# A wait of its own where a matmul pair swaps PSUM banks, a score round moved under it, and row maxima turned by two 64-row transpositions

## The chip, the cores and the metric

The kernel runs on one core of one Trainium2 chip. The metric is the time of one execution in microseconds of the device. The kernel before took 2326.66 us (median of three runs, 2324.75 to 2327.2). Its profiled execution took 2327.55 us.

## The reference

Two blocks work on 2048 tokens of width 576 in float32, and a gate per token mixes them:

```
x = A_x;  g = sigmoid((x * gate_w).sum(-1))
qkv = x @ wqkv                  # 32 heads of width 18
p   = softmax(q k^T * 18**-0.5);   a = (p v) @ wo
y   = layernorm(B_x);  h = gelu(y @ w1 + b1);   b = h @ w2 + b2   # 576 -> 4608 -> 576
out = g * a + (1 - g) * b
```

The attention's input A_x and the perceptron's input B_x are different arrays.

## The kernel before

**Precision and array shapes.** Products are made from float32 parts split in two (`hh` and `hl`, high and low), so that most products take three matmuls. Three shapes of the TensorE array occur in the main loop. Scores and both perceptron products use 64 rows by 128 columns: two matmuls, one on the upper and one on the lower 64 rows, run side by side and write different PSUM banks. The product of probabilities and values (PV, line 268) uses 128 rows by 32 columns. The transposition of line 219 has 128 rows by 32 columns as well.

**The main loop.** There are 32 units (a pair of heads, half of the queries). A unit has 16 steps (`kc`), one for each 128 keys, which makes 512 steps. The maximum of each row of scores must be known before its exponentials, so scores are made twice:

- A *round* (`s1_round`, matmuls on line 202) makes 128x512 scores for two heads, in two banks of the pool `ps_s1`. That pool has three banks, taken in turn. VectorE (DVE) takes each bank's maxima (line 204). A unit has 32 rounds; they run `LEAD` = 4 rounds and a whole unit ahead of the loop.
- When a unit's 32 rounds are done, `s1_finish` (lines 212 to 215) joins the maxima on DVE. `rows` transposes them (line 219), ScalarE (ACT) copies them out of PSUM (line 221), and four DMAs put them as extra rows beside the queries, so that later scores come out with the maximum subtracted.
- `s2` (line 251) makes the scores of one step for one of two blocks of queries, in the one pair of banks of `ps_s2`. ACT takes the exponential (line 253). The next `s2` must wait for that, since there is no second pair of banks.
- `pv` (line 268) multiplies two steps' probabilities with the values, every second step.

**The perceptron as filling.** Between these, `fill` takes pieces from a generator `mlp`: three pieces in two steps, numbered 0 (even step), 1 and 2 (odd step). A generator of `h_pair` makes two chunks of the hidden layer (27 pairs of matmuls on line 489, then DVE line 511 and ACT line 512 read the two banks out and GpSimd and ACT make the GELU). One of `out_pair` makes the second product for 128 tokens (24 pairs on line 614). In `out_pair` the upper 64 rows write bank 0 and the lower 64 rows write bank 1 for 12 pairs (`turn` 0); then they swap (`turn` 1). At that point the kernel calls `nc.tensor.drain()` (line 603), so that no row group writes into a bank that the other is still writing. While rounds last, one `out_pair` is spread over the three pieces as 7, 8 and 9 pairs, so the swap lies inside piece 1, five pairs in. After the last pair, DVE adds the banks to the sum (line 593).

**Order.** The order of instructions on each engine is the order in which the Python code issues them; the pools only add waits. `next_round` issues one round. In an odd step a round stands at the start and one after piece 1; in an even step one stands at the start and one after the second `s2`. Four further rounds stand in steps 2, 4, 6 and 8. Before the loop, `between(n)` issues n stretches of the perceptron, and rounds stand between them.

In what follows R is a round, S an `s2`, V a `pv`, T the transposition, O pairs on line 614, H pairs on line 489.

Of the kernel before, what the change touches and what calls it, by code (L numbers as in the profile page):

```python
# [16 lines left out]
P = 128  # L17
# [11 lines left out]
G = 4  # L29
NFC = F // P  # L30
NG = NFC // G
ND = 288
# [7 lines left out]
LEAD = 4  # L40
# [18 lines left out]
def gated_mix_kernel(ctx: ExitStack, tc: tile.TileContext, x, wqkv, wo, w1, b1, w2, b2, gate_w, out):  # L59
    nc = tc.nc  # L60
# [18 lines left out]
    ident = const.tile([P, P], F32, name="ident")  # L79
# [12 lines left out]
    asm = ctx.enter_context(tc.tile_pool(name="asm", bufs=2))  # L92
    ps_s1 = ctx.enter_context(tc.tile_pool(name="ps_s1", bufs=NS1, space=PSUM))
# [5 lines left out]
    def psum(pool):  # L99
        return pool.tile([P, TB], F32, name="ps")  # L100
# [88 lines left out]

    M4 = {}  # L190

    def s1_round(u, r):


        t, kb = (r % 8, r // 8) if u == 0 else divmod(r, 4)
        if r == 0:
            M4[u] = asm.tile([P, 2, 8, 4], F32, name="m4")
        qa, ka = QA[u % 3], KA[UNITS[u][0] % 3]
        for h in range(2):
            r0 = 64 * h  # L200
            ps = psum(ps_s1)
            nc.tensor.matmul(ps, qa[r0:r0 + 54, t * P:(t + 1) * P], ka[r0:r0 + 54, kb * TB:(kb + 1) * TB],  # L202
                             start=True, stop=True)
            nc.vector.tensor_reduce(M4[u][:, h, t, kb:kb + 1], ps, axis=AX.X, op=ALU.max)  # L204

    def s1_finish(u):

        m4 = M4.pop(u)
        nm = asm.tile([P, 2, 8], F32, name="nm")
        nm2 = asm.tile([P, 2, 2, 8], F32, name="nm2")  # L210
        nmh = asm.tile([P, 2, 8], F32R, name="nmh")
        nc.vector.tensor_reduce(nm, m4, axis=AX.X, op=ALU.max, negate=True)
        nc.vector.tensor_copy(nmh, nm)
        nc.vector.tensor_copy(nm2[:, :, 0, :], nmh.bitcast(F32))
        nc.vector.tensor_tensor(nm2[:, :, 1, :], nm, nmh.bitcast(F32), op=ALU.subtract)

        def rows():
            ps = psum(ps_s1)
            nc.tensor.transpose(ps[:32, :P], nm2.rearrange("p a b c -> p (a b c)"), ident)
            mr = asm.tile([32, P], F32R, name="mr", bufs=1)  # L220
            nc.scalar.activation(mr, ps[:32, :P], AF.Copy)
# [21 lines left out]
    def s2(u, kc, qb):  # L243
        qa, ka = QA[u % 3], KA[UNITS[u][0] % 3]
        n = u * NT + kc
        if n < 2 and qb == 0:
            RING.insert(n, pp.tile([P, 2, 2, TB], F32, name="p"))
        ps = ps_s2.tile([P, 2, TB], F32, name="pss")
        for h in range(2):
            r0 = 64 * h  # L250
            nc.tensor.matmul(ps[:, h, :], ka[r0:r0 + 56, kc * P:(kc + 1) * P], qa[r0:r0 + 56, qb * TB:(qb + 1) * TB],  # L251
                             start=True, stop=True)
        nc.scalar.activation(RING[n % 3][:, qb], ps, AF.Exp, scale=SCALE)  # L253
# [47 lines left out]
    rounds = [(u, r) for u in range(NU) for r in range(NR)]  # L301
    rounds.reverse()

    ROWS = []
    looped = [False]

    def next_round():
        if rounds:
            u, r = rounds.pop()
            s1_round(u, r)  # L310
            if r == NR - 1:
                defer(1, lambda: s1_finish(u))


    def mlp():
        W1, W2, HT = {}, {}, {}
# [148 lines left out]
        def h_pair(q, last, inner=False):  # L465
# [46 lines left out]
            nc.scalar.activation(zs[0], ps[0], AF.Identity, bias=b[0])  # L512
# [70 lines left out]
        def out_pair(i, t, acc):  # L583

            tb, g = seq[i]
            tok = slice(t * P, (t + 1) * P)
            cs = [slice(nn * ND, (nn + 1) * ND) for nn in range(2)]
            bare = not rounds

            def add(ps, base):  # L590
                for nn in range(2):
                    dst = acc[:, t, cs[nn]]
                    nc.vector.scalar_tensor_tensor(dst, ps[nn][:, :ND], 0.5, b2b[:, cs[nn]] if base else dst,  # L593
                                                   op0=ALU.mult, op1=ALU.add)
            ps = [psum(free_pool()) for _ in range(2)]
            ends = {7, 15} if piece[0] == 0 else cuts(24, (3, 2, 1)[piece[0]])
            k = 0
            for turn in range(2):
                if turn == 1 and bare:
                    add(ps, g == 0)  # L600
                    ps = [psum(free_pool()) for _ in range(2)]
                elif turn == 1:
                    nc.tensor.drain()
                for j in ORDER:
                    while (i, j) not in HT:
                        cut[0] = 3
                        yield 0
                    hh, hl = HT[i, j]
                    w_ = ready(W2, (i * (G // 2) + j // 2, j % 2))
                    for h_, p_ in ((hh, 0), (hh, 1), (hl, 0)):  # L610
                        for h in (0, 1) if turn == 0 else (1, 0):
                            r = slice(64 * h, 64 * h + 64)
                            nn = h ^ turn
                            nc.tensor.matmul(ps[nn][:, :ND], h_[r, tok], w_[p_][r, cs[nn]],  # L614
                                             start=(k == 0 or bare and k == 3 * G), stop=(k == 6 * G - 1 or bare and k == 3 * G - 1))
# [419 lines left out]
    RING.append(ring2)  # L1035


    def out_proj():

        OT, BT, done, tmp = {}, {}, {}, {}  # L1040
# [174 lines left out]
    proj = out_proj()  # L1215
    over = [None]
# [29 lines left out]
    for u in range(NU):  # L1246
        for kc in range(NT):
            step = u * NT + kc
            if kc == 1:
                if u + 2 < NU:  # L1250
                    load_q(u + 2)
                if u % 2 == 0 and u // 2 + 1 < NPAIR - 1:
                    load_k(u // 2 + 1)
                    load_v(u // 2 + 1)
                elif u == NU - 5:
                    load_k(NPAIR - 1)
                elif u == NU - 4:
                    load_v(NPAIR - 1)
            at[0] = step

            next_round()
            s2(u, kc, 0)
            run_due(462.0)
            if kc % 2:
                fill(step, 1)
            elif step > 0:
                pv(step - 2)
                while ROWS:
                    ROWS.pop(0)()
                run_due(2080.0)  # L1270
                if step <= 2 * LEAD:
                    next_round()
            else:
                fill(step, 2)
            if kc % 2:
                next_round()
            s2(u, kc, 1)
            if kc % 2 == 0:

                next_round()  # L1280
            run_due(462.0)
            fill(step, 2 if kc % 2 else 0)
    pv(NSTEP - 2)
# [28 lines left out]
```

## Time and profile before

| | |
|---|---|
| time, median of three runs | 2326.66 us (2324.75 to 2327.2) |
| time of the profiled execution | 2327.55 us |
| its span, first to last instruction | 2325.8 us |
| TensorE matmuls | 2295.2 us busy, 99% |
| weight loads | 1615.4 us, 69% |
| DVE | 1663.7 us, 72% |
| ACT | 1379.9 us, 59% |
| GpSimd (POOL) | 947.8 us, 41% |
| matmuls of line 614 | 6912 |
| granted TensorE clock, mean | 0.997 |

PE stands for TensorE's matmuls, PEld for its weight loads. A matmul counts as busy from its start to its modelled end, and several overlap, so 99% does not say that TensorE is at its peak. What counts is how far apart the starts of matmuls lie. In a timeline the columns are start, duration of the merged row, engine, line, operation, output and inputs, form, and the number of instructions; in brackets, the idle time before and what ended it.

### The profile page before, as it was taken

To read this page: it belongs to the slowest core of one execution; us is meant where nothing else is said; L and a number is where in the kernel's file an instruction comes from. 1 tells how busy PE (TensorE), PEld (TensorE's weight loads), DVE (VectorE), ACT (ScalarE), POOL (GpSimd) and SP (SyncE) were. 2 spreads that over 40 slices of the span, in tenths; PEclk is the share of its full clock that TensorE was granted. 3 is DMA by queue.
4 is the path that set the end of the run, shared out by engine and by line. 5 is a ranking of instruction groups with operands and counts; after the bars stand their busy time and mean duration, and the time that the engine had idled before them with its cause. 6 is when DMAs were issued, how large, how long until landed. Compare 5 with 4: busy or idle time off the path is not lost.

```text
span 2325.8 us, 50689 instructions
## 1 busy us (share of the span) xinstructions
PE 2295.2 (99%) x20601; PEld 1615.4 (69%) x20601; DVE 1663.7 (72%) x2921; ACT 1379.9 (59%) x1631; POOL 947.8 (41%) x936
## 2 busy tenths in 40 slices
PE   8999999999999999999999999999999999999999
PEld 7878666666666666666666666666666666666669
DVE  5675777777777777777777777777777777777545
ACT  4223666666666666666666666666666666666662
POOL 4002466566553434443444344434434443333320
PEclk9999899999999999999999999999999999999999
DMA  7756545445473524232263324233364233322346
GB/s 242 247 190 197 175 144 170 157 136 169 139 187 131 164 86 127 96 118 96 90 174 144 114 94 134 81 118 116 118 162 153 94 118 107 106 97 101 113 139 223
DMA packets 160654, 323.58 MB, mean 139 GB/s; under 512 B 56062, under 2 KB 83618, under 8 KB 149586
## 3 DMA queue, kind: packets, MB, share of 16 engines
q1 hardware_dynamic: 156582, 313.57, 43.1%
q10 hardware_dynamic: 3840, 6.78, 0.8%
q8 instruction: 162, 2.65, 0.5%
q14 instruction: 70, 0.57, 0.1%
HBM read 229.07 MB, written 95.16 MB: 139 GB/s over the span
## 4 chain that ended last, share of the span: by engine, by line
PE 90%; POOL 3%; DVE 2%; issue 2%; DMA 1%; ACT 1%; SPq 0%; ACTq 0%; POOLq 0%; DVEq 0%
PE ps L614 20%; PE ps L268 19%; PE ps L489 17%; PE pss L251 12%; PE ps L202 11%; PE ps L880 4%; PE ps L1184 3%; PE ps L898 2%; POOL zz L159 1%; POOL w L159 1%; POOL hl L159 1%; DVE m L204 1%; DMA wraw<-in_B_w_dram 1%; PE ps L795 0%; DMA p<-in_A_wqkv_dram 0%
## 5 line engine op out<-in xcount | busy, mean ns | idle before, releaser
L204 DVE TENSOR_REDUCE m<-ps 128x1 f32<-128x512 f32 x2048 | 1297.3, 684 | 431.2 <-PE ps L202 429.7
L253 ACT ACTIVATE p<-pss 128x1024 f32<-128x1024 f32 x684 | 701.7, 1026 | 456.9 <-PE pss L251 445.3
L489 PE MATMUL ps<-big,w 64*128 64x512 f32 x3834 | 514.8, 392 | 0.1
L614 PE MATMUL ps<-w,hh 64*128 64x288 f32 x4352 | 501.2, 300 | 13.8 <-ACT z L512 2.1
L159 POOL TENSOR_SCALAR zz<-zz 128x512 f32<-128x512 f32 x272 | 169.3, 622 | 827.4 <-ACT zz L575 761.8
L251 PE MATMUL pss<-qa,ka 56*128 56x512 f32 x2048 | 484.1, 437 | 3.8 <-ACT p L253 1.1
L253 ACT ACTIVATE ring<-pss 128x1024 f32<-128x1024 f32 x340 | 348.9, 1026 | 231.4 <-PE pss L251 225.6
L202 PE MATMUL ps<-ka,qa 54*128 54x512 f32 x2048 | 460.8, 410 | 2.8 <-DVE m L204 1.2
L614 PEld LDWEIGHTS ps<-w,hh 64*128 64x128 f32 x4352 | 402.4, 186 | 68.9 <-issue 42.4
L489 PEld LDWEIGHTS ps<-big,w 64*128 64x128 f32 x3834 | 390.1, 185 | 59.6 <-ACT vt L909 0.3
L159 POOL TENSOR_TENSOR zz<-zz,z 128x512 f32<-128x512 f32 x280 | 361.4, 1291 | 35.6 <-ACT zz L577 10.5
L251 PEld LDWEIGHTS pss<-qa,ka 56*128 56x128 f32 x2048 | 198.0, 185 | 254.6 <-ACT p L253 121.4
L614 PE MATMUL ps<-w,hl 64*128 64x288 f32 x2176 | 351.7, 293 | 0.0
L268 PE MATMUL ps<-p,vt 128*32 128x512 f32 x2736 | 344.5, 598 | 0.0
L202 PEld LDWEIGHTS ps<-ka,qa 54*128 54x128 f32 x2048 | 244.5, 185 | 34.0 <-DVE m L204 12.1
L614 PEld LDWEIGHTS ps<-w,hl 64*128 64x128 f32 x2176 | 236.2, 186 | 0.5
L159 POOL TENSOR_TENSOR w<-x,w 128x576 fp32r<-128x576 f32 (+1 forms) x34 | 68.3, 2012 | 308.8 <-ACT w L385 304.6
L159 POOL TENSOR_TENSOR hl<-zz,hh 128x512 fp32r<-128x512 f32 x134 | 174.1, 1300 | 19.0 <-ACT hh L538 8.1
L268 PE MATMUL ps<-ring,vt 128*32 128x512 f32 x1360 | 179.1, 598 | 0.0
L268 PEld LDWEIGHTS ps<-p,vt 128*32 128x32 f32 x2736 | 71.4, 109 | 147.3 <-issue 147.3
L593 DVE SCALAR_TENSOR_TENSOR x<-ps,x 128x288 f32<-128x288 f32 x270 | 110.8, 452 | 29.8 <-PE ps L614 16.4
L880 PE MATMUL ps<-big,wqk 128*128 128x512 f32 x504 | 123.4, 399 | 0.1
(122 smaller groups left out, 1403.3 us busy)
## 6 DMA issues: line engine op xcount, KB each, us to landing
w<-w_scr SPq DMA_DIRECT2D x54, 1152.0 KB
w<-w_scr SPq DMA_DIRECT2D x108, 576.0 KB
w_scr<-w SPq DMA_DIRECT2D x18, 1152.0 KB
w_scr<-w SPq DMA_DIRECT2D x36, 576.0 KB
qa<-qk_scr SPq DMA_DIRECT2D x192, 72.0 KB
ka<-qk_scr SPq DMA_DIRECT2D x90, 144.0 KB
x<-in_B_w_dram SPq DMA_DIRECT2D x34, 288.0 KB
qk_scr<-hh SPq DMA_DIRECT2D x36, 256.0 KB
```

What stands on the lines that cost most here:

```text
L159: fn(*args, **kw)
L202: nc.tensor.matmul(ps, qa[r0:r0 + 54, t * P:(t + 1) * P], ka[r0:r0 + 54, kb * TB:(kb + 1) * TB], start=True, stop=True)
L204: nc.vector.tensor_reduce(M4[u][:, h, t, kb:kb + 1], ps, axis=AX.X, op=ALU.max)
L251: nc.tensor.matmul(ps[:, h, :], ka[r0:r0 + 56, kc * P:(kc + 1) * P], qa[r0:r0 + 56, qb * TB:(qb + 1) * TB], start=True, stop=True)
L253: nc.scalar.activation(RING[n % 3][:, qb], ps, AF.Exp, scale=SCALE)
L268: nc.tensor.matmul(OB[u][r:r + 32, :], v[:, k, 19 * h:19 * h + 32], RING[c % 3][:, qb, h, :], start=(k == 0), stop=(k == NT - 1))
L489: nc.tensor.matmul(ps[h], wt[w_][r, c, :], Y[s_][r, c, :], start=(k == 0), stop=(k == 26))
L593: nc.vector.scalar_tensor_tensor(dst, ps[nn][:, :ND], 0.5, b2b[:, cs[nn]] if base else dst, op0=ALU.mult, op1=ALU.add)
L614: nc.tensor.matmul(ps[nn][:, :ND], h_[r, tok], w_[p_][r, cs[nn]], start=(k == 0 or bare and k == 3 * G), stop=(k == 6 * G - 1 or bare and ...
L880: nc.tensor.matmul(ps, w_[:, c, ms], big[:, s_, :], start=(k == 0), stop=(k == len(prods) - 1))
L898: nc.tensor.matmul(ps[:, :ND], big[:, s_, tok], w_[:, c, cs], start=(k == 0), stop=False)
L1184: nc.tensor.matmul(ps[t, n][:, :ND], OT[b][3][:, s_, tok], w_part(w_, c)[:, cs], start=(c == 0 and k == 0), stop=(c == 4 and k == 1))
```

## The change

1. In `out_pair` the drain at the swap goes. The two last matmuls of turn 0 each add one to a semaphore `turn_sem`, and the first matmul of turn 1 waits for both. Just before that wait a round is issued (`lend_round`), if the swap isn't the end of a piece; the next round that the loop would issue is then left out (`loop_round`). This happens at all 137 swaps.
2. The maxima of a unit lie in one 128x128 tile with the values that `s1_finish` makes. Inside the loop, `rows` makes two transpositions, one for each 64 partitions, in the shape of the scores (64 rows by 128 columns), into two banks of `ps_s1`. DVE copies the 32 rows that matter out of each (line 224 of the kernel after). It is issued after the second `s2` of the even step, no longer after `pv`. One unit of 32, the one before the loop, is done as before.
3. One stretch of the perceptron fewer stands in the first `between`, and two rounds stand in place of the last `between(1)`. Of the four further rounds in steps 2 to 8, those in steps 6 and 8 go. Of the chunk pair number 2, DVE takes both read-outs (before, ACT took one).

```diff
     def rows():
-        ps = psum(ps_s1)
-        nc.tensor.transpose(ps[:32, :P], nm2.rearrange("p a b c -> p (a b c)"), ident)
         mr = asm.tile([32, P], F32R, name="mr", bufs=1)
-        nc.scalar.activation(mr, ps[:32, :P], AF.Copy)
+        if looped[0]:
+            for h in range(2):
+                half(mr, h)
+            store_rows(mr)
...
+    def half(mr, h):
+        r = slice(64 * h, 64 * h + 64)
+        ps = psum(ps_s1)
+        nc.tensor.transpose(ps[:, :64], nm2[r, :], ident[r, r])
+        nc.vector.tensor_copy(mr[:, r], ps[:32, :64])
...
+    def lend_round():
+        if rounds and not lent[0]:
+            next_round()
+            lent[0] = 1
+
+    def loop_round():
+        if lent[0]:
+            lent[0] = 0
+        else:
+            next_round()
...
-            nc.scalar.activation(zs[0], ps[0], AF.Identity, bias=b[0])
+            if q == 2:
+                nc.vector.tensor_scalar(zs[0], ps[0], b[0], None, op0=ALU.add)
+            else:
+                nc.scalar.activation(zs[0], ps[0], AF.Identity, bias=b[0])
...
                 elif turn == 1:
-                    nc.tensor.drain()
+                    if 3 * G not in ends:
+                        lend_round()
+                    turned[0] += 2
+                    nc.tensor.wait_ge(turn_sem, turned[0])
...
+                            if k == 3 * G - 1:
+                                mm.then_inc(turn_sem, 1)
...
-        between(6 if len(rounds) == NU * NR - NR else 2)
+        between(5 if len(rounds) == NU * NR - NR else 2)
         next_round()
         run_due(233.0)
-    between(1)
+    for part in range(2):
+        next_round()
+        run_due(500.0)
...
                 pv(step - 2)
-                while ROWS:
-                    ROWS.pop(0)()
                 run_due(2080.0)
-                if step <= 2 * LEAD:
+                if step <= LEAD:
                     next_round()
...
             s2(u, kc, 1)
+            while kc % 2 == 0 and ROWS:
+                ROWS.pop(0)()
             if kc % 2 == 0:
-                next_round()
+                loop_round()
```

Every other `next_round` of the loop's steps becomes `loop_round` too.

The first place is the swap in an `out_pair` of the main loop, on TensorE. In the kernel before (`ps` takes the second product's banks on line 614 and the scores' banks on line 202; `pss` are the banks of `s2`), with the drain, which the listing leaves out, between the second and the third row:

```order
L614 MATMUL ps<-w_10902,hh 128x288 x4
L614 MATMUL ps<-w_10902,hl 128x288 x2
L614 MATMUL ps<-w_10898,hh 128x288 x4
L614 MATMUL ps<-w_10898,hl 128x288 x2
L202 MATMUL ps<-ka_108,qa_105 128x512 x2
L251 MATMUL pss<-qa_103,ka_107 128x512 x2
L614 MATMUL ps<-w_10900,hh 128x288 x4
```

On TensorE at such a swap in the kernel after, with the semaphores that are waited for:

```order
L650 MATMUL ps<-w_13221,hh 128x288 x4
L650 MATMUL ps<-w_13221,hl 128x288 x2
L205 MATMUL ps<-ka_107,qa_105 128x512 [waits DVE_49] x2
L650 MATMUL ps<-w_13217,hh 128x288 [waits turn]
L650 MATMUL ps<-w_13217,hh 128x288 x3
L650 MATMUL ps<-w_13217,hl 128x288 x2
L268 MATMUL pss<-qa_103,ka_106 128x512 [waits Activation_49]
```

The round has moved three pairs forward, to the swap, and the first matmul behind it waits for `turn`.

The second place is the transposition in an even step, on TensorE, in the kernel before (`ident` is the identity, `nm` the joined maxima, the first two rows are the second half of V and T):

```order
L268 MATMUL ps<-ring_2268,vt_109 32x512 x4
L219 MATMUL ps<-ident,nm_13710 32x128 [waits DVE_49]
L251 MATMUL pss<-qa_103,ka_106 128x512 [waits Activation_49]
L251 MATMUL pss<-qa_103,ka_106 128x512
L202 MATMUL ps<-ka_107,qa_105 128x512 [waits DVE_49] x2
```

And in the kernel after, where S stands first and the two transpositions stand right ahead of a round:

```order
L285 MATMUL ps<-p,vt_110 32x512 x8
L268 MATMUL pss<-qa_105,ka_107 128x512 [waits Activation_49]
L268 MATMUL pss<-qa_105,ka_107 128x512
L223 MATMUL ps<-ident,m_24780 128x64 [waits DVE_49] x2
L205 MATMUL ps<-ka_108,qa_104 128x512 [waits DVE_49] x2
```

T has moved behind S, takes two banks of `ps_s1` where it took one, and its round follows at once.

The third place is the start of the loop on TensorE. In the kernel before, from the end of chunk pair 2 (line 489) on:

```order
L489 MATMUL ps<-big,w_2206 128x512 x12
L202 MATMUL ps<-ka_106,qa_104 128x512 x2
L489 MATMUL ps<-big,w_2206 128x512 x6
L614 MATMUL ps<-w_2051,hh 128x288 x4
L614 MATMUL ps<-w_2051,hl 128x288 x2
L614 MATMUL ps<-w_2058,hh 128x288 x4
L202 MATMUL ps<-ka_106,qa_104 128x512 x2
L614 MATMUL ps<-w_2058,hl 128x288 x2
L202 MATMUL ps<-ka_106,qa_104 128x512 x2
L251 MATMUL pss<-qa_103,ka_106 128x512 x2
```

In the kernel after, from the same point on:

```order
L519 MATMUL ps<-big,w_2206 128x512 x12
L205 MATMUL ps<-ka_106,qa_104 128x512 x8
L268 MATMUL pss<-qa_103,ka_106 128x512 x2
L650 MATMUL ps<-w_2051,hh 128x288 x4
L650 MATMUL ps<-w_2051,hl 128x288 x2
L650 MATMUL ps<-w_2058,hh 128x288 x4
L650 MATMUL ps<-w_2058,hl 128x288 x2
L650 MATMUL ps<-w_2098,hh 128x288 x4
L650 MATMUL ps<-w_2098,hl 128x288 x2
```

Four rounds now stand between the chunk pair and the first `out_pair`, where none stood; the first `out_pair` then runs nine pairs in a row.

More of the change, by code (lines that the diff above doesn't have):

```diff
@@ L190, in gated_mix_kernel, with maxima @@
     M4 = {}
+    def maxima(t):
+        return t[:, 64:].rearrange("p (a b c) -> p a b c", a=2, b=8)
     def s1_round(u, r):
@@ L196, in s1_round @@
         if r == 0:
-            M4[u] = asm.tile([P, 2, 8, 4], F32, name="m4")
+            M4[u] = asm.tile([P, P], F32, name="m4")
         qa, ka = QA[u % 3], KA[UNITS[u][0] % 3]
@@ L312, in next_round @@
                 defer(1, lambda: s1_finish(u))
+    lent = [0]
+    def lend_round():
[7 more added lines that the diff above has]
+            next_round()
     def mlp():
@@ L511, in h_pair @@
             nc.vector.tensor_scalar(zs[1], ps[1], b[1], None, op0=ALU.add)
-            nc.scalar.activation(zs[0], ps[0], AF.Identity, bias=b[0])
+            if q == 2:
+                nc.vector.tensor_scalar(zs[0], ps[0], b[0], None, op0=ALU.add)
+            else:
+                nc.scalar.activation(zs[0], ps[0], AF.Identity, bias=b[0])
             for h in (1, 0):
@@ L613, in out_pair @@
                             nn = h ^ turn
-                            nc.tensor.matmul(ps[nn][:, :ND], h_[r, tok], w_[p_][r, cs[nn]],
-                                             start=(k == 0 or bare and k == 3 * G), stop=(k == 6 * G - 1 or bare and k == 3 * G - 1))
+                            mm = nc.tensor.matmul(ps[nn][:, :ND], h_[r, tok], w_[p_][r, cs[nn]],
+                                                  start=(k == 0 or bare and k == 3 * G), stop=(k == 6 * G - 1 or bare and k == 3 * G - 1))
+                            if bare:
+                                continue
+                            if k == 3 * G - 1:
+                                mm.then_inc(turn_sem, 1)
+                                tc.no_tile_sem_insts.add(mm.ins.name)
+                                tc.add_to_no_dep_group(f"turn{turned[0]}", mm.ins)
+                            elif k == 3 * G and h == 0:
+                                tc.declare_fence(mm.ins, group=f"turn{turned[0] - 2}")
                         k += 1
@@ L1035, in gated_mix_kernel @@
     RING.append(ring2)
+    turn_sem = tc.alloc_semaphore("turn")
+    turned = [0]
     def out_proj():
@@ L1275, in gated_mix_kernel @@
             if kc % 2:
-                next_round()
+                loop_round()
             s2(u, kc, 1)
+            while kc % 2 == 0 and ROWS:
+                ROWS.pop(0)()
             if kc % 2 == 0:
-                next_round()
+                loop_round()
             run_due(462.0)
```

21 lines of the change are left out of this document (13 added, 8 removed).

## The prediction

> **What bounds the kernel now.** I read the page first: the span, the engines' busy shares, the clock, the chain that ended last, and the group of the maxima.
>
> ```profile
> span 2325.8 us, 50689 instructions
> PE 2295.2 (99%) x20601; PEld 1615.4 (69%) x20601; DVE 1663.7 (72%) x2921; ACT 1379.9 (59%) x1631; POOL 947.8 (41%) x936
> PEclk9999899999999999999999999999999999999999
> PE 90%; POOL 3%; DVE 2%; issue 2%; DMA 1%; ACT 1%; SPq 0%; ACTq 0%; POOLq 0%; DVEq 0%
> L204 DVE TENSOR_REDUCE m<-ps 128x1 f32<-128x512 f32 x2048 | 1297.3, 684 | 431.2 <-PE ps L202 429.7
> ```
>
> TensorE carries 90% of the chain, so time between its matmuls counts nearly one to one. DVE waits 431 us for rounds and has room. Since overlapping matmuls hide gaps, I next read the waits of the weight loads, and the drain's own line.
>
> ```profile
> PEld pss L251 <- ACT p L253: 121.4, 229, 1.4
> PEld ps L614 <- issue: 42.4, 137, 0.4
> L603 PEldq DRAIN  x137: 875/1188/1912, 256.3 to 2191.0; - x137
> ```
>
> There are 137 drains and 137 idle times before line 614 that no engine explains: 42.4/137 = 0.31 us each, so all are alike. The first row warns that S often waits for its exponential; 1.03 us of ACT stand between one S and the next.
>
> **The swap.** Now the timeline around one drain, TensorE, then ACT, then DVE.
>
> ```profile
> 1022.72 0.51 PE L202 MATMUL ps<-ka,qa 54*128 54x512 f32 x2
> 1022.95 0.52 PE L251 MATMUL pss<-qa,ka 56*128 56x512 f32 x2
> 1023.51 0.49 PE L614 MATMUL ps<-w,hh 64*128 64x288 f32 x4
> 1023.77 0.35 PE L614 MATMUL ps<-w,hl 64*128 64x288 f32 x2
> 1024.21 0.53 PE L614 MATMUL ps<-w,hh 64*128 64x288 f32 x4
> 1024.57 0.30 PE L614 MATMUL ps<-w,hl 64*128 64x288 f32 x2
> 1024.70 0.40 PE L202 MATMUL ps<-ka,qa 54*128 54x512 f32 x2
> 1024.94 0.41 PE L251 MATMUL pss<-qa,ka 56*128 56x512 f32 x2
> 1025.17 0.44 PE L614 MATMUL ps<-w,hh 64*128 64x288 f32 x4
> 1025.44 0.30 PE L614 MATMUL ps<-w,hl 64*128 64x288 f32 x2
> ```
>
> ```profile
> 1023.56 1.02 ACT L253 ACTIVATE p<-pss 128x1024 f32<-128x1024 f32 x1 [0.71 <-PE pss L251]
> ```
>
> ```profile
> 1021.99 2.49 DVE L204 TENSOR_REDUCE m<-ps 128x1 f32<-128x512 f32 x4
> 1025.14 1.29 DVE L204 TENSOR_REDUCE m<-ps 128x1 f32<-128x512 f32 x2 [0.67 <-PE ps L202]
> ```
>
> Undisturbed, two pairs take 0.27 us (1025.17 to 1025.44): 0.13 each. At the swap the last pair starts by 1023.82 (its two matmuls are 0.05 apart, 0.35 against 0.30), the third pair behind it at 1024.57: 0.75 where three pitches are 0.40. A drain costs 0.35 us: 0.25 until weights load again and 0.10 because the first load is not hidden (0.36 from 1024.21 to 1024.57 against 0.27). Times 137 that is 48 us.
>
> After: the last pair ends 0.30 after its start, at 1024.12. The semaphore must reach TensorE: 0.04 is what DVE needed (a round ends at 1025.10, DVE starts at 1025.14), and 0.09 what the drain needed (1024.12 to 1024.21). Then 0.10 of load: the next pair can stream at 1024.26 to 1024.31. Meanwhile the moved round takes its 0.24 (1024.70 to 1024.94), from 1023.95 to 1024.19. So 0.07 to 0.12 of the 0.35 stay, and TensorE alone would gain 0.23 to 0.28. The Trainium skill ("TensorE: Matmul & The Clock Gate", section "The cost: per-tile semaphore tail") says that increments serialize, about 25 + 4.7 per tile + 26.3 ns per increment; for two tiles with two increments I estimate 0.09 us from it, the upper end here. No run here shows two increments yet, and by that page this gain would be 0.23 us.
>
> Behind the waiting matmul stands everything on TensorE, S first, and ACT waits for S. On DVE the round's maxima stay ahead of the two sums of line 593, as before. The round also waits for DVE itself: its second bank is free after the third of the four maxima, near 1023.86 (2.49/4 = 0.62 each), 0.09 before it is due. With 0.05 and a load of 0.10 it starts 0.06 late, which the swap's own wait covers.
>
> S is the next to be late. It now comes 0.36 after its exponential ended (1024.94 against 1024.58). What S needs at least shows where it is bound:
>
> ```profile
> 253.18 1.02 ACT L253 ACTIVATE p<-pss 128x1024 f32<-128x1024 f32 x1 [0.68 <-PE pss L251]
> 254.26 0.79 PE L251 MATMUL pss<-qa,ka 56*128 56x512 f32 x2 [0.87 <-ACT p L253]
> ```
>
> 0.06 from the end of ACT to S, and 0.10 for its load: S streams at 1024.74 at the earliest. So of 0.23 to 0.28 only about 0.20 arrive, and I take 0.20: 27 us. Ends: 0.13 (ACT holds something else) and 0.28, so 18 to 38 us.
>
> **The transposition.** One of 31, TensorE, then ACT and DVE:
>
> ```profile
> 1128.04 1.04 PE L268 MATMUL ps<-p,vt 128*32 128x512 f32 x8
> 1129.01 0.28 PE L219 MATMUL ps<-ident,nm 128*32 128x128 f32 x1
> 1129.23 0.50 PE L251 MATMUL pss<-qa,ka 56*128 56x512 f32 x2
> 1129.57 0.40 PE L202 MATMUL ps<-ka,qa 54*128 54x512 f32 x2
> 1129.80 0.43 PE L614 MATMUL ps<-w,hh 64*128 64x288 f32 x4
> ```
>
> ```profile
> 1129.34 0.27 ACT L221 ACTIVATE mr<-ps 32x128 fp32r<-32x128 f32 x1 [0.97 <-PE ps L219]
> ```
>
> ```profile
> 1127.14 0.17 DVE L214 COPY nm<-nmh 128x16 f32<-128x16 f32 x1
> 1128.04 1.28 DVE L204 TENSOR_REDUCE m<-ps 128x1 f32<-128x512 f32 x2
> ```
>
> T takes 0.22 in line (1129.01 to 1129.23), and the round behind it finds two free banks. After: S at 1129.01; both halves at 1129.35, side by side, 64 columns where 128 took 0.22, so 0.11 by my estimate; the round at 1129.46. But of three banks the round before took A and B, the halves take C and A, and the round gets B and C. Its second matmul must wait until DVE has copied the first half out of C: end of the half 1129.52 (0.28 less 0.11), 0.04, a copy of 0.17 to 0.27 (the DVE and ACT copies above), 0.06 and a load of 0.10: it streams near 1129.94, and the next pair follows at 1130.18 instead of 1129.80. That is 0.38 lost, 31 times 12 us. Where the round is late already, as here,
>
> ```profile
> 1005.74 1.05 PE L202 MATMUL ps<-ka,qa 54*128 54x512 f32 x2
> ```
>
> (1.05 against 0.40, DVE being behind), little is lost, and S coming 0.22 sooner gives a bit back. I know no share for these two kinds, so I take the middle, 6 us lost, with the ends 0 and 12. The 31 ACT copies go and 62 DVE copies come; DVE's 431 us of waiting cover them. T's four DMAs go out on SP's queue about a microsecond later:
>
> ```profile
> 1005.80 2.73 SPq L113 DMA_DIRECT2D qa<-mr  x4
> ```
>
> Their issue takes 2.73 us, and the next unit's S, which reads those rows, comes four steps on, eight exponentials of 1.02 us at least; so that costs nothing.
>
> **The start of the loop.** Windows (length, busy time and count of PE, PEld, DVE, ACT, POOL, then the granted clock, DMA share, GB/s), then two waits:
>
> ```profile
> 245.60:249.00 3.40, 1.49 (x12) 0.68 (x8) 2.24 (x4) 3.19 (x7) 3.25 (x4) 1.00 0.15 57
> 249.00:252.40 3.40, 3.13 (x17) 2.50 (x19) 1.22 (x3) 3.34 (x7) 3.35 (x3) 0.50 0.44 136
> 252.40:255.80 3.40, 2.53 (x14) 1.77 (x12) 1.55 (x4) 1.83 (x3) 2.50 (x2) 0.50 0.58 148
> 255.80:259.20 3.40, 3.32 (x20) 2.48 (x20) 2.20 (x4) 2.49 (x4) 1.28 (x1) 0.50 1.09 156
> 259.20:262.60 3.40, 3.40 (x27) 3.12 (x26) 1.48 (x3) 2.17 (x3) 0.00 (x0) 0.50 0.57 79
> ```
>
> ```profile
> 249.15 0.85 PE L614 MATMUL ps<-w,hh 64*128 64x288 f32 x4 [2.06 <-ACT z L512]
> 266.10 0.49 PE L202 MATMUL ps<-ka,qa 54*128 54x512 f32 x1 [0.31 <-DVE m L204]
> ```
>
> TensorE idles 2.06 us, and the granted clock is 0.50 for the next 13.6 us. After, four rounds stand in that place, and DVE reads both z first (about 0.7 each), so the second round waits some 1.8 us and the eight maxima take 8 x 0.62 = 5 us. That is no denser than the 1.49 of 3.40 us that went before the fall, so I expect the half clock again; denser pieces follow it. I take 1 us gained, ends 4 lost to 5 gained. The two rounds that leave steps 6 and 8 save their stall (0.31 idle and 0.10 of load, last row): 1 us.
>
> **Sum.** 27 - 6 + 1 + 1 = 23 us: 2327.55 - 23 = 2304.5 for the profiled execution, which lay 0.9 above the median; 2326.66 - 23 = 2303.7 for the median. The forecast's own range is 2288 to 2317 (the ends do not all meet). A measurement of this kernel can tell about 0.2%, 4.7 us, from no change.
>
> **Rivals.** *ACT takes the gain.* If ACT mostly holds a GELU step (0.62 us) when S comes sooner, three swaps in four gain nothing: 7 - 6 + 2 = 3 us, 2324. For: S waits for ACT 229 times. Against: ACT is 59% busy, and idle 0.71 before that exponential. *All of it arrives.* S is not bound, T's copy is hidden, the clock holds: 38 + 1 + 5 = 44, 2283. *The clock alone holds.* The largest gap is 1.8 us, under 2.06, and the half clock's cost goes, 5 us instead of 1: 2300. Against stands that a window with 1.49 of 3.40 us busy was enough for the fall. The Trainium skill (same page, section "Why this matters for your kernels") asks only for no gaps over about 3 us, so by it the clock would hold; this trace disagrees, since 2.06 us sufficed. *Slower: the moved round blocks TensorE.* It stands 0.09 behind DVE. If DVE is one maximum later (0.62) there, its second matmul streams at 1024.63, and the pair behind it at 1024.87; before, that pair streamed at 1024.31 with the round's 0.24 still to come, 1024.55. So each swap loses 0.32: 44 us; with 6 lost at T and 2 gained as above, 2375. It decides from a lag of 0.3 us on. Against: the maxima at the swap run back to back in every out_pair alike.
>
> **Chances.** Forecast 0.70, all arrives 0.08, clock 0.08, ACT takes it 0.07, slower 0.07. Faster by over 0.2%: 0.85; within 0.2%: 0.08; slower: 0.07. The range 2284 to 2318 leaves out the first and last rivals and the edges.
>
> **What would show it.** Right: no idle time "issue" on line 650; the pair behind a swap 0.45 us after the last instead of 0.40 plus a round; S about 0.15 behind ACT at swaps; a DVE release before the second matmul behind T. Wrong: rounds at swaps waiting for DVE, S at swaps as far from its predecessor as before, or the gain found at the loop's start alone.

## The result and the profile after

| | before | after |
|---|---|---|
| time, median of six runs each | 2326.65 us (2324.75 to 2327.97) | 2308.24 us (2306.44 to 2309.39) |
| ratio, 95% interval | | 0.992 (0.9908 to 0.9933) |
| time of the profiled execution | 2327.55 us | 2308.79 us |
| its span | 2325.8 us | 2307.0 us |

The change makes the kernel 18.4 us faster; 23 had been forecast. In the kernel after, R stands on line 205, S on 268, V on 285, T on 223, the pairs of `out_pair` (O) on 650, the maxima on 207 and the exponential on 270.

The page of the kernel after, the lines that answer to those shown of before: span, chain, group of the maxima.

```profile
span 2307.0 us, 50654 instructions
PE 87%; DVE 4%; POOL 3%; issue 2%; DMA 2%; ACT 2%; SPq 0%; ACTq 0%; POOLq 0%; DVEq 0%
L207 DVE TENSOR_REDUCE m<-ps 128x1 f32<-128x512 f32 x2048 | 1285.9, 683 | 329.3 <-PE ps L205 321.1
```

TensorE still carries the chain, at 87% where it was 90%. DVE's wait for rounds fell from 431 to 329 us: it is less far ahead of TensorE than it was. Next the waits of the weight loads (us in total, times, longest).

```profile
PEld pss L268 <- ACT p L270: 138.2, 249, 1.6
PEld ps L205 <- DVE mr L224: 6.4, 20, 0.3
PEld ps L650 <- PE ps L650: 2.3, 14, 0.2
```

The 137 idle times before the pairs that nothing explained (42.4 us) are gone; of the longer idle times that this view lists, 2.3 us are left, now with a releaser, TensorE itself. Two waits have grown or are new: S for its exponential (121.4 us before, 138.2 now) and R for DVE's copy of T's half, 20 times.

**A swap after**, TensorE, then ACT and DVE, from the timeline:

```profile
1015.69 0.51 PE L650 MATMUL ps<-w,hh 64*128 64x288 f32 x4
1015.96 0.37 PE L650 MATMUL ps<-w,hl 64*128 64x288 f32 x2
1016.09 0.54 PE L205 MATMUL ps<-ka,qa 54*128 54x512 f32 x2
1016.39 0.53 PE L650 MATMUL ps<-w,hh 64*128 64x288 f32 x4
1016.76 0.30 PE L650 MATMUL ps<-w,hl 64*128 64x288 f32 x2
1016.89 0.46 PE L268 MATMUL pss<-qa,ka 56*128 56x512 f32 x2
```

```profile
1015.76 1.03 ACT L270 ACTIVATE p<-pss 128x1024 f32<-128x1024 f32 x1 [0.72 <-PE pss L268]
```

```profile
1014.19 3.68 DVE L207 TENSOR_REDUCE m<-ps 128x1 f32<-128x512 f32 x6
```

The last pair before the swap starts by 1016.04 (its two matmuls are 0.08 apart) and ends at 1016.33; the first one behind it starts at 1016.39, 0.35 later (0.45 was forecast), with the round in between. The third pair behind the swap follows at 1016.76, 0.72 after the last, where before it took 0.75 without a round. S starts 0.10 after its exponential ends (1016.89 against 1016.79); before, that was 0.36. By the single records DVE is done with the round's second bank, the third of these six maxima, at 1016.08, and the round's second matmul starts at 1016.17, 0.13 after the last pair. At all of 133 swaps that distance is 0.13, so DVE doesn't hold the round.

Over 133 swaps (all but the first four), the last pair before the swap and the second pair behind the next S are 1.473 us apart before and 1.262 after: 0.211 less.

**A transposition after**, TensorE, then DVE:

```profile
1119.29 1.04 PE L285 MATMUL ps<-p,vt 128*32 128x512 f32 x8
1120.26 0.50 PE L268 MATMUL pss<-qa,ka 56*128 56x512 f32 x2
1120.60 0.22 PE L223 MATMUL ps<-ident,m 64*128 64x64 f32 x2
1120.62 0.99 PE L205 MATMUL ps<-ka,qa 54*128 54x512 f32 x2
1121.12 0.64 PE L650 MATMUL ps<-w,hh 64*128 64x288 f32 x3
1121.49 0.29 PE L650 MATMUL ps<-w,hl 64*128 64x288 f32 x1
```

```profile
1120.85 0.34 DVE L224 CAST mr<-ps 32x64 fp32r<-32x64 f32 x2 [0.81 <-PE ps L223]
```

Both halves cost almost nothing in line (1120.60, the round at 1120.62). But the round's two matmuls span 0.99 us instead of 0.40: the first starts at once, the second at 1121.12 by the single records, 0.06 after the first of DVE's two overlapping copies ends (1120.85 and 0.21). The pair behind starts on the upper rows at 1121.12 too, and on the lower ones only 0.24 later. From then on the two row groups run out of step, which is why the rows that follow are merged as x3 and x1.

**The start of the loop after**, windows (length, busy time and count of PE, PEld, DVE, ACT, POOL, granted clock, DMA share, GB/s):

```profile
247.40:250.80 3.40, 1.70 (x12) 0.81 (x8) 3.28 (x7) 3.20 (x7) 3.25 (x4) 1.00 0.12 37
250.80:254.20 3.40, 3.31 (x13) 2.32 (x15) 3.40 (x6) 1.99 (x4) 3.40 (x4) 0.55 0.55 170
254.20:257.60 3.40, 3.04 (x22) 2.32 (x20) 1.22 (x3) 1.84 (x3) 0.95 (x1) 0.50 0.78 191
257.60:261.00 3.40, 3.40 (x25) 3.23 (x26) 2.72 (x5) 3.10 (x5) 1.28 (x1) 0.50 0.93 118
```

The clock falls here as it did before: to half, for some 10 us, three such windows (before, 13.6 us, four windows).

**Where the 18.8 us of the two profiled executions lie.** By the 21st V both kernels have started the same matmuls (250 of R, 170 of S, 576 of O, 486 of the hidden layer; 12 swaps), and again by the 241st (123 more swaps, 28 more T). Of before, then of after:

```profile
426.54 1.05 PE L268 MATMUL ps<-p,vt 128*32 128x512 f32 x6
2154.90 1.07 PE L268 MATMUL ps<-p,vt 128*32 128x512 f32 x8
```

```profile
425.29 1.06 PE L285 MATMUL ps<-p,vt 128*32 128x512 f32 x8
2135.67 0.64 PE L285 MATMUL ps<-p,vt 128*32 128x512 f32 x4
```

Up to the 21st V: 1.25 us gained. From there to the 241st: 1728.36 against 1710.38, 17.98 gained. The rest of the span, 170.9 against 171.3, loses 0.4; two swaps and the last T lie in it.

### The profile page after: what moved, and what is told of

Same layout as the page of the kernel before. It is cut to its first block, busy times and chain, and to the rows that moved or that the text cites. A ratio compares the mean times of both kernels' runs of the same rounds, so it can differ in the third digit from the quotient of the medians.

```text
span 2307.0 us, 50654 instructions
## 1 busy us (share of the span) xinstructions
PE 2282.2 (99%) x20632; PEld 1619.7 (70%) x20632; DVE 1667.5 (72%) x2984; ACT 1372.1 (59%) x1599; POOL 947.1 (41%) x936
## 4 chain that ended last, share of the span: by engine, by line
PE 87%; DVE 4%; POOL 3%; issue 2%; DMA 2%; ACT 2%; SPq 0%; ACTq 0%; POOLq 0%; DVEq 0%
PE ps L285 18%; PE ps L650 18%; PE ps L519 17%; PE pss L268 12%; PE ps L205 11%; PE ps L924 5%; PE ps L1231 2%; PE ps L942 2%; DVE m L207 2%; POOL zz L159 1%; POOL w L159 1%; DMA w_scr<-w 1%; POOL hl L159 1%; PE ps L839 1%; ACT p L270 1%
## 5 line engine op out<-in xcount | busy, mean ns | idle before, releaser
L205 PE MATMUL ps<-ka,qa 54*128 54x512 f32 x2048 | 492.3, 414 | 7.4 <-DVE m L207 5.0
L268 PE MATMUL pss<-qa,ka 56*128 56x512 f32 x2048 | 490.2, 442 | 5.3 <-ACT p L270 2.6
L268 PEld LDWEIGHTS pss<-qa,ka 56*128 56x128 f32 x2048 | 200.5, 184 | 283.5 <-ACT p L270 138.2
L205 PEld LDWEIGHTS ps<-ka,qa 54*128 54x128 f32 x2048 | 269.5, 185 | 45.8 <-DVE m L207 13.3
```

## The experiments

Each was timed against the kernel before on the same chip, whose medians there were 2326.32 (first four), 2327.12 (next four) and 2325.68 us (last two).

**T as before.** All three parts stay, but T is again one transposition behind V with ACT's copy. The edit in short:

```diff
-    maxima in one 128x128 tile; rows(): two half(mr, h), behind the second s2
+    rows(): one transpose into ps[:32, :P], nc.scalar.activation(mr, ...), behind pv
```

> The kernel after with the row maxima turned as before: one 128x32 transposition behind V, copied by ACT. My theory (the two halves cost 0.22 us more each time, through the third bank of the scores, 31 times) expects 7 us less than the kernel after: 2301 us, and no round that waits for a copy of the row maxima. The rival (the shape of the scores saves a change of the array's shape, so the halves are a gain) expects 2308 us or more, up to 2315.

Measured: 2298.76 us (2297.5 to 2299.66), ratio 0.9881 (0.9868 to 0.9895). So the turning by halves costs some 9 us of what the rest gains, 2 more than expected, and the rival that it saves something falls. Of the 9, 1.6 us are the stall of a store, which comes last in this section.

**The semaphore without the round.**

```diff
                 elif turn == 1:
-                    if 3 * G not in ends:
-                        lend_round()
                     turned[0] += 2
                     nc.tensor.wait_ge(turn_sem, turned[0])
```

> The kernel after without the moved round: the semaphore alone stands at the swap, with nothing under it. My theory (the gain is the round's 0.24 us under the wait; the semaphore by itself is at most 0.05 us cheaper than the drain) expects 22 to 29 us more than the kernel after: 2330 to 2337 us. The rival (the semaphore is cheap and the drain was dear, wherever the round stands) expects 2308 to 2313 us.

Measured: 2330.86 us (2329.26 to 2334.36), ratio 1.0021 (1.0011 to 1.003), 22.6 more than the kernel after, as the theory had it. A swap of this kernel on TensorE:

```profile
1024.68 0.36 PE L648 MATMUL ps<-w,hl 64*128 64x288 f32 x2
1025.10 0.53 PE L648 MATMUL ps<-w,hh 64*128 64x288 f32 x4
1025.47 0.30 PE L648 MATMUL ps<-w,hl 64*128 64x288 f32 x2
```

The last pair starts by 1024.75; the first behind it follows 0.35 later and the third 0.72, just as in the kernel after, only with no round in that time. Over 133 swaps it is 1.456 us where the drain took 1.473. A semaphore of its own in place of a drain is worth 0.02 us; what gains is the work put under it.

**The round with the drain.** The increments of `turn_sem` go as well.

```diff
                         lend_round()
-                    turned[0] += 2
-                    nc.tensor.wait_ge(turn_sem, turned[0])
+                    nc.tensor.drain()
```

> The kernel after with the drain in place of the semaphore, and the round still moved ahead of it. My theory (a drain also waits for the round, so nothing is hidden: 0.35 us from the round's last matmul on, as before) expects 27 to 30 us more than the kernel after: 2335 to 2338 us. The rival (the round's new place helps DVE or ACT by itself) expects 2308 to 2320 us.

Measured: 2344.63 us (2342.06 to 2345.23), ratio 1.008 (1.0066 to 1.0094): in the expected direction, 7 us further.

```profile
1019.16 0.35 PE L649 MATMUL ps<-w,hl 64*128 64x288 f32 x2
1019.28 0.52 PE L205 MATMUL ps<-ka,qa 54*128 54x512 f32 x2
1019.91 0.53 PE L649 MATMUL ps<-w,hh 64*128 64x288 f32 x4
```

A drain waits for the round as well: the round ends at 1019.80, and the pairs come 0.11 after that (0.11 at all of 133 swaps). It then costs the round's whole 0.52 us, not the 0.24 that it takes among other matmuls. The average from the last pair to the second pair behind S is 1.553 us, 0.08 more than in the kernel before; 137 times that is 11 us, and with T's price it makes the 18. The first part needs both, the semaphore and the moved round.

**The old start.** The third part alone is undone, in short:

```diff
-        between(5 if ...); two rounds in place of between(1); if step <= LEAD; DVE reads out both z
+        between(6 if ...); between(1); if step <= 2 * LEAD; ACT reads out z[0]
```

> The kernel after with the start of the loop as before (six stretches ahead, the last stretch, four further rounds in steps 2 to 8, ACT reading one z of chunk pair 2). My theory (the half clock falls in either start, and the start is worth about 1 us) expects 2309 us, between 2307 and 2311, with the granted clock at 0.50 for four windows again. The rival (part 3 carries a good share of the gain) expects 2314 us or more.

Measured: 2307.49 us (2304.63 to 2307.84), ratio 0.9916 (0.9903 to 0.993). Within what can be told, the new start gives nothing. The four windows of half clock that were expected didn't come: the profile of this run has one, from 256.4 to 259.8 us.

**The halves behind V.**

```diff
                 pv(step - 2)
+                while ROWS:
+                    ROWS.pop(0)()
...
-            while kc % 2 == 0 and ROWS:
-                ROWS.pop(0)()
```

> The changed kernel with the transposition T put back directly behind V: its two 64-row halves and DVE's copies stay, but the second S now stands between them and the round. Theory (the 9.5 us that the halves cost against the old transposition come from the place: the round's second matmul follows a half whose third bank DVE has still to copy): with an S of 0.23 us and more between them, most of that wait goes and about 4 us of the 9.5 come back, 2304 (2301 to 2306). Rival (the place and its bank cost nothing; the two extra small matmuls and DVE's 62 copies do): 2308, as the changed kernel. Second rival (the place behind the S was a gain, since ACT gets its S sooner there): 2311 and more, since S comes 0.2 us later 31 times.

Measured: 2303.0 us (2301.6 to 2305.16), ratio 0.9899 (0.9885 to 0.9912), as the theory had it. The same T as above, on TensorE:

```profile
1115.96 1.04 PE L285 MATMUL ps<-p,vt 128*32 128x512 f32 x8
1116.94 0.28 PE L223 MATMUL ps<-ident,m 64*128 64x64 f32 x2
1117.02 0.47 PE L268 MATMUL pss<-qa,ka 56*128 56x512 f32 x2
1117.34 0.68 PE L205 MATMUL ps<-ka,qa 54*128 54x512 f32 x2
```

The round comes 0.4 after the halves instead of 0.02, and its second matmul is late by 0.2 at most (0.68 against 0.47 to 0.50 of an S or R run side by side). From the 21st to the 241st V this kernel takes 1704.88 us, 5.5 less than the kernel after; 1.6 of that is the store's stall, which is missing here, so 3.9 are the bank's. From this V to the next, 17 of 31 such stretches are within 0.03 us of those of the old transposition; in the kernel after, the same stretch at such a place is 0.28 longer. Where DVE is behind, the halves lose 0.1 to 0.5 in this place too.

**The old T in the new place.** The place behind the second `s2` stays; in short:

```diff
-    maxima in one 128x128 tile; rows(): two half(mr, h)
+    rows(): one transpose into ps[:32, :P], nc.scalar.activation(mr, ...)
             while kc % 2 == 0 and ROWS:
                 ROWS.pop(0)()
```

> The changed kernel with T as one 128-row transposition with ACT's copy, as in the kernel before, but at the new place, behind the second S and directly ahead of the round. Theory (bank: the two halves take the banks that the round behind them needs): one transposition takes one bank of three and the round finds two free, its price in line is 0.22 us as before, so 2300 (2298 to 2303), near the old T at the old place (2299). Rival (place: a change of the array's shape in front of the round costs, whatever the banks): 2305 to 2309.

Measured: 2301.81 us (2301.29 to 2303.4), ratio 0.9895 (0.988 to 0.991).

```profile
1115.30 1.04 PE L268 MATMUL ps<-p,vt 128*32 128x512 f32 x8
1116.27 0.50 PE L251 MATMUL pss<-qa,ka 56*128 56x512 f32 x2
1116.70 0.28 PE L219 MATMUL ps<-ident,nm 128*32 128x128 f32 x1
1116.91 0.50 PE L202 MATMUL ps<-ka,qa 54*128 54x512 f32 x2
1117.26 0.44 PE L633 MATMUL ps<-w,hh 64*128 64x288 f32 x4
```

The time lies where the theory put it, but its reason holds by half only. The round runs undisturbed (0.50), so the bank is no matter here; yet T stands 0.43 behind S, where a round stands 0.33 to 0.34 behind an S, and the pair 0.35 behind the round, where it was 0.24. Two changes of shape more, 0.1 each: that the change of shape is what takes this time is argued from the order. From this V to the next it makes about 0.20 us at 19 of the 21 T's whose round is in time, and under 0.1 at six of the nine others, 4.0 us in all; the whole run loses 3 us to the old place. The change avoids these with its halves and pays 0.28 for the bank instead.

**A shorter exponential ahead of the swap**, in the kernel after, and as a control in the kernel before:

```diff
-        nc.scalar.activation(RING[n % 3][:, qb], ps, AF.Exp, scale=SCALE)
+        w = 448 if kc % 2 and qb == 0 and looped[0] and n > 64 else TB
+        nc.scalar.activation(RING[n % 3][:, qb, :, :w], ps[:, :, :w], AF.Exp, scale=SCALE)
```

> The changed kernel with one exponential in four shortened: that of the first block of each odd step, the one behind which the S of a swap stands, covers 2x448 of its 2x512 columns, some 0.12 us less on ACT; the last 64 columns of each half keep what an older step left there. Theory (behind a swap the S is now bound by its exponential, so that what ACT does there sets 0.05 of each swap): 0.04 to 0.07 us less at 137 swaps, so 5 to 9 us less, plus what stretches without swaps give, which the same edit on the kernel before shows by itself: 2300 (2297 to 2304). Rival (TensorE's own wait bounds the swap, S has room): 2307 to 2309.

> The kernel before with the same one exponential in four shortened by 64 of 512 columns in each half; the same part is left out. It is the control for the shortened exponential in the changed kernel. Theory (at a drain the S has 0.36 us of room behind its exponential, so ACT sets nothing there): 2325 (2322 to 2327), the difference being what stretches without swaps give. Rival (ACT sets the pace at drains too): 2317 to 2320.

Measured: after 2301.96 us (2300.26 to 2304.98), ratio 0.9895 (0.9881 to 0.9908), so 6 us less than the change; before 2324.54 us (2321.55 to 2325.84), ratio 0.9989 (0.998 to 0.9998), some 2.6 less. A swap of the changed kernel with it, ACT, then TensorE:

```profile
1011.04 0.92 ACT L271 ACTIVATE p<-pss 128x896 f32<-128x896 f32 x1 [0.72 <-PE pss L268]
```

```profile
1012.02 0.29 PE L651 MATMUL ps<-w,hl 64*128 64x288 f32 x2
1012.16 0.40 PE L268 MATMUL pss<-qa,ka 56*128 56x512 f32 x2
```

S comes 0.20 after its exponential and 0.14 after the pair before it. In the kernel after it starts as close to that pair, 0.13 on average in both; what its exponential held back shows behind its start, where the next pair follows at 0.28 on average and here at 0.24. The average of 133 swaps falls from 1.262 to 1.224 us, while in the kernel before it stays at 1.473 (1.472). So ACT sets 0.04 of a swap in the kernel after and nothing in the kernel before. The forecast's claim that S becomes bound by ACT is shown. The sizes: less the control's 2.6 the times leave 3.7 us for the swaps, where 5 to 9 were expected; from the 21st to the 241st V the profiles give 7.1 and 2.5, so 4.6 for 123 swaps.

**The swap alone**: old T and old start, the fastest version of all. The edit's main lines (the increments and `loop_round` come with them):

```diff
-                    nc.tensor.drain()
+                    if 3 * G not in ends:
+                        lend_round()
+                    turned[0] += 2
+                    nc.tensor.wait_ge(turn_sem, turned[0])
```

> The kernel before with the first part of the change alone: semaphore and moved round at the 137 swaps; the old transposition and the old start of the loop (with the further rounds in steps 6 and 8 and ACT reading out both the chunk pairs) are back. Theory (the swap gives some 0.207 us each, as the runs with the old transposition show between their 20th and 240th V, and the new start gives nothing): 137 x 0.207 = 28 us under the kernel before, 2298 to 2299 (2296 to 2300), the same as the run with the old transposition and the new start. Rival (the new start is worth the 2 us that were forecast for it): 2301 (2300 to 2302).

Measured: 2297.86 us (2296.58 to 2300.22), ratio 0.9882 (0.9867 to 0.9897), 27.8 us under the kernel before. Its 21st and 241st V:

```profile
422.79 0.64 PE L268 MATMUL ps<-p,vt 128*32 128x512 f32 x4
2124.69 0.64 PE L268 MATMUL ps<-p,vt 128*32 128x512 f32 x4
```

1701.90 us against 1728.36: 26.5 over 123 swaps, 0.215 each. It beats the kernel before and the changed kernel; from the run with the old T (2298.76) it can't be told apart.

**No store of T's rows on ACT's queue.** In two of 31 units the stores of T's rows stand on ACT's queue. One of them in the kernel after holds up an exponential; ACT's queue and ACT, then TensorE:

```profile
1194.80 0.65 ACTq L113 DMA_DIRECT2D qa<-mr  x1
1195.50 1.02 ACT L270 ACTIVATE p<-pss 128x1024 f32<-128x1024 f32 x1 [2.95 <-PE ps L205]
```

```profile
1196.58 0.51 PE L268 MATMUL pss<-qa,ka 56*128 56x512 f32 x2 [1.31 <-ACT p L270]
```

Against the old T, the stretch from V to V at this place is 1.6 us longer, the one place of the whole loop with such a difference; the old start and the short exponential, with their halves behind S too, have it as well (1.2 and 1.5); the runs with the halves behind V or with the old T don't, nor do the two in which nothing is hidden at the swap (the semaphore without the round, the round with the drain).

```diff
-            aside = slot[0] < ybusy[0]
+            aside = False
```

> The changed kernel with the stores of T's rows always on SP's queue (in two of the 31 units they stand on ACT's queue, and one of those waits there 1.6 us for another transfer, ahead of an exponential). Theory: the stall of 1.6 us near 1195 us goes and nothing takes its place, 2306.5 (2305 to 2308); in the profile no exponential there is over 1 us late. Rival: SP's queue is busy with the loads of the perceptron's input just then, the rows come late and the S that reads them waits longer than 1.6 us: 2309 and more.

Measured: 2311.39 us (2310.21 to 2311.99), ratio 0.9938 (0.9926 to 0.9951): the rival. SP's queue, then TensorE:

```profile
1185.59 7.16 SPq L113 DMA_DIRECT2D qa<-mr  x4
```

```profile
1198.89 1.12 PE L268 MATMUL pss<-qa,ka 56*128 56x512 f32 x2 [3.98 <-DMA qa<-mr]
```

On SP's queue four such stores take 7.16 us here (2.73 elsewhere), and S waits 3.98 us for the rows. The two units stand where the perceptron's input is loaded. The gap of 3.98 us costs more than itself: the windows from 1197.4 to 1200.8 and from there to 1204.2 have a granted clock of 0.51 and 0.50, and the stretch from the next V to the one behind it is 2.05 us longer than with the old T.

What the store on ACT's queue waits for in the kernel after can be read from the trace's semaphore events. The one that is late is the fourth of its unit, and its landing is told by the same semaphore as that of the first, which ACT issued at 1186.41. ACT's queue waits for that first store to land; its last event comes at 1194.43, the wait ends at 1194.45, and the fourth store is issued at 1194.80. In the run with the semaphore without the round the same wait is for a transfer that had landed 6.2 us before ACT came to it (1196.41 against 1202.61).

## Why the prediction was right, step by step

The time came out within the forecast's range because its largest term, the swap, was right in its mechanism and nearly in its size. The smaller terms missed by several us.

**The swap** (27 us gained by the prediction, ends 18 to 38). Right: 0.211 us at each swap by the trace, 28.9 for 137, and 27.8 by the run with the swap alone. Its steps:

- TensorE's own gain was put at 0.23 to 0.28. The third pair comes at 0.72 instead of 0.74 on average and holds the round's 0.24: 0.26. The semaphore reached TensorE 0.06 after the last matmul's end (1016.33 to 1016.39), and the forecast's 0.10 for the first load didn't appear there but at the next pair, which follows at 0.24 instead of 0.13. The sum came out; the place of this load was wrong. By the Trainium skill ("TensorE: Matmul & The Clock Gate", section "The cost: per-tile semaphore tail") the estimate was 0.09 for the two increments; this trace shows 0.06 from the modelled end of the last matmul, with the transfer to the next matmul included, and so does the run without the round.
- "S is the next to be late" was right. S was given 0.16 behind its exponential. It starts 0.115 behind it on average, and the shortened exponential shows that 0.04 more is held back behind that start: 0.16 together. So 0.21 arrives where 0.20 was taken.
- The moved round isn't held up by DVE, so the rival on the slower side has no place in this trace; nor does ACT take the gain.

**The transposition** (6 us lost, ends 0 to 12). The mechanism of the bank was right, the size too small, and a second cost was put at nothing: 7.4 us lie between the 21st and 241st V (the run with the old T needs 1702.95 us there, the change 1710.38) and some 9 over the whole run by the medians. Its steps, one by one:

- "The next pair follows at 1130.18", 0.38 lost where the round is in time. It is 0.28: the pair's upper half doesn't wait for the round's late second matmul to finish, it starts with it (both 1121.12), and only the lower half is late.
- "Where the round is late already, little is lost": right. With the old T the round's second matmul is late, by 0.12 us and more, at 9 of 30 T's, and at seven of these the halves take only 0.12 to 0.16 more (the other two, 0.5 more and 0.5 less, cancel).
- "I know no share for these two kinds, so I take the middle": this was the weak step, and that 6 came near is in part luck. 21 of 30 rounds are in time, more than half, but each costs 0.28 and not 0.38: 21 x 0.28 and 9 x 0.14 are 7.1 us. Added up one by one, the 30 stretches from V to V are 6.7 longer, and the last T, with no round behind it, takes 0.4.
- "So that costs nothing", of the four DMAs: right in all but one unit, where a store on ACT's queue holds up an exponential for 1.6 us. The prediction looked at SP's queue and not at the second queue that `aside` chooses. With it T takes some 8.7.

The expected DVE release before the second matmul is there, 20 times in 31.

**The start and the two rounds** (1 + 1 us gained). Not found. With the old start the change takes 2307.49 instead of 2308.24, and with the old T 2297.86 instead of 2298.76; both differences point the same way and are too small to be told from nothing. In the two profiled executions 1.25 us are gained up to the 21st V, of which 12 swaps make 2.5 and two T's take 0.3: 1.0 is lost there. But this can't be put down to the start. The run without stores on ACT's queue has the same instructions up to that V as the kernel after and starts it at 422.57 us instead of 425.29, with one window of half clock where the kernel after has three. With one window each, the old start (422.94) and the new one (422.57) lie 0.4 apart. The step that has no support is "denser pieces follow it": TensorE waits 1.64 us for the maxima of four rounds in a row, and whether that eats what the denser pairs give was not separated. What the two rounds gave by themselves wasn't measured either. That the half clock comes again was right, and the rival that the clock holds was wrong: the gap was 1.64 us, under the 1.8 forecast, and the clock fell all the same. The Trainium skill (same page, section "Why this matters for your kernels") asks for no gaps over some 3 us; this trace disagrees a second time.

**The sum.** 28.9 us gained at the swaps, 8.7 lost at T (6.7, 0.4 and the store's 1.6), 1.0 lost up to the 21st V and 0.5 behind the 241st that neither swaps nor T explain: 18.7 us, where the profiled executions differ by 18.8. The 0.5 lies within chance, since other kernels with the same instructions behind the 241st V differ there by a microsecond (171.3 to 172.4). Against the forecast's 23, the swaps gave 2 us more, T took 2.7 more, and the start, the two rounds and the end of the span came out 3.5 lower; so one miss covers part of the others.

## What to carry to other kernels

A wait costs little or nothing less for being on a semaphore instead of a drain; it is won by putting work under it that the wait doesn't cover (a drain covers that work too), and then the next engine in line must be looked at, since it caps the gain. A piece that is turned to a cheaper shape is cheap in line only if the banks it takes aren't those that the very next instruction needs: leave one unrelated piece between them. When a step moves, look at every queue that its transfers can take, also the one used in only a few units: a wait on a queue that an engine shares holds up that engine.

## What the runs showed of the hardware

The half clock at the start of the loop doesn't last equally long from one execution to the next. With the same start, it was 0.50 for some 10 us in the kernel after (above), but in the run with the old T:

```profile
250.80:254.20 3.40, 3.10 (x17) 2.34 (x18) 3.16 (x6) 2.01 (x4) 3.40 (x4) 0.72 0.53 165
254.20:257.60 3.40, 2.85 (x23) 2.27 (x22) 1.59 (x3) 1.89 (x4) 0.55 (x1) 0.78 0.79 163
```

Here 0.28 and 0.22 of two windows are missing, one window of 3.4 us at half. Over the profiles of these runs it was one, two, three or four such windows, and one and three with the same start. Two executions with the same instructions, one window in one and three in the other, lie 2.7 us apart at the 21st V (422.57 and 425.29, above). The Trainium skill ("TensorE: Matmul & The Clock Gate", section "What's actually happening") says of a kernel's first microseconds that the gate's window runs freely, so that the same kernel has more or fewer slow matmuls from run to run; these profiles show a like spread in the middle of a kernel. That the window's place is its cause here is not shown.

Two row groups that have come out of step stay so for a while. Behind the T above, on TensorE (each matmul of a round or an S is a row of its own here):

```profile
1122.15 0.39 PE L205 MATMUL ps<-ka,qa 54*128 54x512 f32 x1
1122.38 0.39 PE L268 MATMUL pss<-qa,ka 56*128 56x512 f32 x1
1122.39 0.40 PE L205 MATMUL ps<-ka,qa 54*128 54x512 f32 x1
```

The two halves of a round start 0.24 us apart, where undisturbed ones start 0.01 apart, and those of the next round, at 1123.28 and 1123.53, still do. The first half of S even starts before the second half of the round that stands ahead of it in the program.
